# The opening of a fused attention and FFN kernel: loads in order of use, batch 0 in spare PSUM banks, dummy matmuls, FFN1 beside batch 1, and an ELU that reads PSUM once on VectorE

## The chip, the cores and the metric

One core of one Trainium2 chip. The metric is the device time of one execution in microseconds (us). Times are medians of several executions. The profile is that of one execution; its span runs from the first to the last instruction of the program and is about 2 us shorter than the device time.

"Clock" is the mean granted clock of TensorE, as a share of full speed.

## The reference

Attention over 8 batches, 8 heads, 576 queries of width 64, with 16 extra "beacon" keys and values in front of each sequence; causal for the ordinary keys. Its output, reshaped to 4608 tokens by 512, goes through a two-layer FFN with an ELU.

```python
k_all = concatenate([beacon_k, k], axis=2);  v_all = concatenate([beacon_v, v], axis=2)
scores = where(causal, -1e9, matmul(q, k_all.T) / sqrt(64))        # [8, 8, 576, 592]
a = softmax(scores);  attn = matmul(a, v_all)
x = attn.transpose(0, 2, 1, 3).reshape(4608, 512)
h = x @ w_in                                                        # 512 -> 2048
g = where(h > 0, h, exp(minimum(h, 0)) - 1)                         # ELU
out = g @ w_out                                                     # 2048 -> 512
```

## The kernel before

The heads of a batch are worked two at a time, as four "pairs". For a pair there are four steps: `T` transposes q and k on TensorE and copies them out of PSUM, `SC` makes a group of scores (four groups per pair, each with its Exp of 128x832 on ScalarE and its causal masks on VectorE), `AV` makes the product with v and, with a matrix of ones, the row sums, and normalises: ln and exp(-x) of the sums on ScalarE, then a multiply on VectorE. `AVR` does the last 64 queries of all four pairs.

The FFN takes tiles of 512 tokens. The kernel is a software pipeline: in a period, the attention of batch b, FFN1 of tile b-1 and FFN2 of tile b-2 are dealt out in 16 steps. Batch 0 has a period for itself, since no tile is ready; the next has batch 1 and FFN1 of tile 0; from then on all three run together. The instructions of an engine stand in the order of these calls, so the order of the calls is the schedule.

The kernel's PSUM tiles take eight banks: tag `S` two buffers of two banks, `hps` (FFN1) two of one, `ops` (FFN2) two of one.

```python
def T(b, p):
    t = psum.tile([P, 2, 1024], BF16, tag="S")
    ...                                      # 24 transposes of q and k into t
    nc.scalar.copy(out=qT..., in_=t[:, 0, 0:S]...)
    nc.scalar.copy(out=kT..., in_=t[:, 1, 0:S]...)

def AV(b, p):
    a = psum.tile([P, 2, 512], FP32, tag="S")
    av_mms(b, p, 0, Q1, a[:, 0, 0:Q1], a[:, 1, 0:Q1], True)   # v and ones by turns
    recip(rl, a[:, 1, 0:Q1])                                  # ScalarE: Ln, then Exp(-x)
    nc.vector.tensor_tensor(out=xT..., in0=a[:, 0, 0:Q1], in1=rl, op=ALU.mult)

def slots_of(b):
    for p in range(NP):
        sl.append(lambda p=p: (SC(b, p, 0), SC(b, p, 1)))
        sl.append(lambda p=p: (SC(b, p, 2), SC(b, p, 3)))
        sl.append(lambda p=p: (T(b, p + 1), AV(b, p)))        # last pair: AV, AVR
    if b + 1 < B: sl.append(lambda: T(b + 1, 0))

def ffn1(t, fc):
    ...                                      # 4 matmuls into hps
    nc.scalar.activation(out=e, in_=hps, func=AFT.Exp)
    nc.vector.tensor_scalar(out=r, in0=hps, scalar1=0.0, op0=ALU.max)
    nc.vector.scalar_tensor_tensor(out=gt, in0=e, scalar=1.0, in1=r,
                                   op0=ALU.subtract, op1=ALU.min)
# cut: loads, masks, ffn2, the loop over the periods
```

The softmax here doesn't subtract the row's maximum and nothing guards it: scores larger than these inputs give would overflow.

Of the kernel before, what the change touches and what calls it, by code (L numbers as in the profile page):

```python
# [17 lines left out]
def kernel(  # L18
# [11 lines left out]
    nc = tc.nc  # L30
# [80 lines left out]
    def load_v(b):  # L111
        v16 = st[b][2]
        nc.gpsimd.dma_start(
            out=v16[0:NB, 0, :, :], in_=beacon_v[b].rearrange("h n d -> n h d"))
        for j in range(NKC):
            r0 = NB if j == 0 else 0
            n = kc[j] - r0
            nc.gpsimd.dma_start(
                out=v16[r0:r0 + n, j, :, :],
                in_=v[b, :, ilo[j]:ilo[j] + n, :].rearrange("h s d -> s h d"),  # L120
            )

    bk32 = konst.tile([P, H, D], FP32)
    for b in range(B):
        nc.sync.dma_start(  # L125
            out=bk32[NB * b:NB * (b + 1), :, :],
            in_=beacon_k[b].rearrange("h n d -> n h d"))
    new_stage(0)
    load_qk(0, 0, 2)
    identb = konst.tile([P, P], BF16)  # L130
    make_identity(nc, identb)
    load_qk(0, 2, 4)
    triu = konst.tile([P, 2, P], FP16)
# [5 lines left out]
    ones = konst.tile([P, D], FP16)  # L139
    nc.gpsimd.memset(ones, 1.0)  # L140
    NKT = 3
    kTs = [konst.tile([P, P * NKC], BF16, name=f"kT{i}") for i in range(NKT)]
    for kt in kTs:
        nc.gpsimd.memset(kt[:, SK:P * NKC], 0.0)
    load_v(0)
    load_qk(0, 4, 8)
# [3 lines left out]
    new_stage(1)  # L150
    load_qk(1, 0, H)
    load_v(1)
# [3 lines left out]
    bkst = konst.tile([P, H, D], BF16)  # L156
    nc.vector.tensor_copy(out=bkst, in_=bk32)


    bkT = konst.tile([P, NP, P], BF16)  # L160

    def beacon_T():
        tb = psum.tile([P, 2, 1024], BF16, tag="S", name="tb")
        for p in range(NP):
            nc.tensor.transpose(
                out=tb[:, 0, P * p:P * (p + 1)], in_=bkst[:, 2 * p:2 * p + 2, :], identity=identb)
        nc.vector.tensor_copy(out=bkT, in_=tb[:, 0, 0:NP * P])
# [4 lines left out]
    def T(b, p):  # L172
        qst, kst, _ = st[b]
        t = psum.tile([P, 2, 1024], BF16, tag="S", name="tp")
        for i, src in ((0, qst), (1, kst)):
            for r in range(R):
                for h in range(2):
                    nc.tensor.transpose(  # L178
                        out=t[D * h:D * (h + 1), i, PR * r:PR * (r + 1)],
# [3 lines left out]
        qT = attn.tile([P, S], BF16, tag="qT")  # L183
        kT = kTs[(b * NP + p) % NKT]
        nc.vector.tensor_copy(out=kT[:, 0:NB], in_=bkT[:, p, NB * b:NB * (b + 1)])
        nc.scalar.copy(  # L186
            out=qT.rearrange("c (p r) -> c p r", r=R),
            in_=t[:, 0, 0:S].rearrange("c (r p) -> c p r", r=R))
        nc.scalar.copy(
            out=kT[:, NB:SK].rearrange("c (p r) -> c p r", r=R),  # L190
            in_=t[:, 1, 0:S].rearrange("c (r p) -> c p r", r=R))
        qkT[(b, p)] = (qT, kT)

    def SC(b, p, g):
        qT, kT = qkT[(b, p)]
        if g == 0:
            ets[(b, p)] = attn.tile([P, 2, ECOLS], FP16, tag="et", bufs=6, name="et")
        et = ets[(b, p)]
        s = psum.tile([P, 2, 512], FP32, tag="S", name="sc")
        c0, c1 = GW * g, GW * (g + 1)  # L200
# [24 lines left out]
    def av_mms(b, p, qa, qe, u, l, first):  # L225
        v16 = st[b][2]
        et = ets[(b, p)]
        for j in range(NKC):
# [5 lines left out]
            for dst, isl in ((u, False), (l, True)):  # L234
                for h in range(2):
                    nc.tensor.matmul(  # L236
                        out=dst[D * h:D * (h + 1), a - qa:qe - qa],
                        lhsT=ones[0:kc[j], :] if isl else v16[0:kc[j], j, 2 * p + h, :],
                        rhs=et[0:kc[j], h, ca:ce],
                        start=(first and j == 0),  # L240
                        stop=(j == NKC - 1 or ilo[j + 1] >= qe),
                        skip_group_check=True,
                    )

    def recip(o, i):
        nc.scalar.activation(out=o, in_=i, func=AFT.Ln, bias=0.0, scale=1.0)  # L246
# [122 lines left out]
```

## Time and profile before

| | before |
|---|---|
| median of 4 runs | 402.39 us (401.84 to 402.59) |
| span of the profiled run, clock | 400.2 us, 0.981 |
| TensorE, VectorE, ScalarE busy | 371.9, 282.4, 263.9 us |
| first transpose, first Exp of the scores | 9.38, 12.93 us |
| first FFN1 matmul of tile 0, of tile 1 | 43.55, 77.33 us |
| a period in the steady state | 41.75 us |

The engine names in the profile are PE for TensorE (PEld for its weight loads), ACT for ScalarE, DVE for VectorE and POOL for GpSimd.

The first view is the windows of the kernel before: each row is a stretch of time (from:to, its length), then the busy time of each engine with the number of its instructions, the granted clock, the DMA share and GB/s. I cut the stretches at the first Exp of each pair of batch 0, at the first FFN1 matmul of tile 0 and of tile 1, and at the end of the first full period.

```profile
core 0: us, PE busy (x) PEld busy (x) DVE busy (x) ACT busy (x) POOL busy (x), PEclk, DMA share, GB/s
12.93:20.01 7.08, 5.28 (x60) 3.53 (x57) 1.38 (x6) 5.44 (x8) 4.83 (x7) 1.00 1.21 176
20.01:27.63 7.62, 4.63 (x60) 3.51 (x60) 2.26 (x7) 5.54 (x10) 2.64 (x3) 0.78 1.25 206
27.63:34.92 7.29, 4.49 (x60) 3.28 (x60) 2.07 (x7) 5.53 (x9) 1.84 (x3) 0.77 1.61 189
34.92:43.55 8.63, 6.73 (x138) 5.64 (x138) 2.78 (x8) 5.26 (x9) 4.18 (x7) 0.60 1.51 196
43.55:77.33 33.78, 29.53 (x386) 15.38 (x385) 27.84 (x61) 31.38 (x52) 10.21 (x13) 1.00 1.05 122
77.33:119.08 41.75, 41.75 (x449) 20.85 (x448) 32.09 (x65) 32.02 (x51) 6.26 (x8) 1.00 0.59 69
```

The last row is the steady state: TensorE is busy in all of 41.75 us. The four pairs of batch 0 take 7 to 8.6 us each, in which TensorE is busy 4.5 to 6.7 us and ScalarE 5.3 to 5.5: neither is full, so waits bound the pairs. The clock falls to 0.60 there. With FFN1 of tile 0 beside batch 1, ScalarE is busy 31.4 of 33.8 us.

The second view is the timeline of ScalarE (start, length, engine, line, operation, output<-input, shapes, count; in brackets the idle time ahead and what ended it) between pair 0 and pair 1.

```profile
18.85 0.60 ACT L246 ACTIVATE rl<-av 128x512 f32<-128x512 f32 x1 [1.10 <-PE av L236]
19.48 0.63 ACT L247 ACTIVATE rl<-rl 128x512 f32<-128x512 f32 x1
20.01 0.84 ACT L216 ACTIVATE et<-sc 128x832 f16<-128x832 f32 x1
21.30 2.38 ACT L216 ACTIVATE et<-sc 128x832 f16<-128x832 f32 x3 [0.44 <-PE sc L208]
```

The second score group comes late: its Exp starts 1.29 us after the first, where the next follow at 0.76. Its bank of tag `S` held the product of pair 0 until VectorE's multiply had read it, which ended at 20.83. (The profile names the first Exp as what the scores waited for, since it ended 0.02 later.)

From the page's list of groups (busy us, mean ns of one | idle before, releaser): the two VectorE passes of the ELU, and the q copy on ScalarE.

```profile
L295 DVE TENSOR_SCALAR r<-hps 128x512 f16<-128x512 f32 x144 | 99.2, 689 | 23.1 <-ACT e L293 21.2
L297 DVE SCALAR_TENSOR_TENSOR gt<-e,r 128x512 f16<-128x512 f32 x144 | 99.7, 692 | 4.9
...
L186 ACT COPY qT<-tp 128x576 bf16<-128x576 bf16 x32 | 20.6, 643 | 25.0 <-PE tp L178 25.0
```

### The profile page before, as it was taken

What the parts mean: (1) busy time and instruction counts of PE and PEld (TensorE: products, weight loads), DVE (VectorE), ACT (ScalarE), POOL (GpSimd) and SP (SyncE); (2) the same over time, 40 slices, a digit from 0 to 9 for tenths busy, and PEclk for the clock granted to TensorE, in tenths of its full rate; (3) what the DMA queues carried; (4) which work ended last, traced back from release to release, by engine and by line L of the source; (5) the groups of instructions that cost most, each with busy time, mean ns of one, the idle gap of its engine ahead of it and who ended that gap; (6) DMA issues with size and microseconds to landing.
All of it is one profiled execution on the core that took longest, in us unless ns stands there. A gap on an engine that the chain in (4) does not pass through costs nothing.

```text
span 400.2 us, 8907 instructions
## 1 busy us (share of the span) xinstructions
PE 371.9 (93%) x3716; PEld 189.0 (47%) x3716; DVE 282.4 (71%) x558; ACT 263.9 (66%) x417; POOL 60.4 (15%) x88
## 2 busy tenths in 40 slices
PE   0656989999999999999999999999999999999996
PEld 0444644444554445444545454555455544444442
DVE  0132578977777777777787787777777788888841
ACT  1676899688758885788668875887588843333300
POOL 8734301400140014001400131000000000000000
PEclk9986899999999999999999999999999999999999
DMA  9999996900890079104950288000000001010112
GB/s 108 162 205 186 205 123 93 89 0 28 144 91 29 28 122 105 33 28 86 119 59 26 54 132 76 28 29 26 28 29 12 18 35 45 27 54 26 52 54 79
DMA packets 61864, 28.75 MB, mean 72 GB/s; under 512 B 40832, under 2 KB 57216, under 8 KB 61824
## 3 DMA queue, kind: packets, MB, share of 16 engines
q0 software_dynamic: 55488, 18.49, 41.8%
q1 hardware_dynamic: 6336, 9.70, 6.5%
q8 instruction: 29, 0.48, 0.5%
q14 instruction: 11, 0.09, 0.1%
HBM read 37.22 MB, written 9.44 MB: 117 GB/s over the span
## 4 chain that ended last, share of the span: by engine, by line
PE 87%; ACT 8%; DVE 2%; DMA 1%; SPq 1%; issue 0%; DVEq 0%
PE ops L309 31%; PE hps L288 31%; PE av L236 10%; PE sc L208 7%; PE tp L178 5%; ACT et L216 4%; PE avr L236 3%; DMA bk_82<-in_beacon_k_dram 1%; ACT rl L247 1%; ACT e L293 1%; ACT rl L246 1%; ACT qT L186 1%; SPq L125 1%; DVE xT L254 1%; DVE r L295 0%
## 5 line engine op out<-in xcount | busy, mean ns | idle before, releaser
L288 PE MATMUL hps<-xT,w_in_80 128*128 128x512 f16 x576 | 148.6, 381 | 1.0 <-DVE r L295 1.0
L309 PE MATMUL ops<-w_out_81,gt 128*128 128x512 f16 x576 | 145.2, 379 | 0.0
L293 ACT ACTIVATE e<-hps 128x512 f32<-128x512 f32 x144 | 86.2, 599 | 59.3 <-PE hps L288 58.0
L216 ACT ACTIVATE et<-sc 128x832 f16<-128x832 f32 x128 | 103.6, 862 | 18.6 <-PE sc L208 18.6
L295 DVE TENSOR_SCALAR r<-hps 128x512 f16<-128x512 f32 x144 | 99.2, 689 | 23.1 <-ACT e L293 21.2
L297 DVE SCALAR_TENSOR_TENSOR gt<-e,r 128x512 f16<-128x512 f32 x144 | 99.7, 692 | 4.9
L309 PEld LDWEIGHTS <-gt 128*128 128x128 f16 x576 | 56.3, 98 | 68.0
L288 PEld LDWEIGHTS <-w_in_80 128*128 128x128 f16 x576 | 48.9, 98 | 57.1 <-issue 6.3
L222 DVE TENSOR_TENSOR et<-et,triu 128x256 f16<-128x256 f16 (+2 forms) x160 | 39.4, 273 | 20.9 <-ACT et L216 20.7
L254 DVE TENSOR_TENSOR xT<-av,rl 128x512 f16<-128x512 f32 x32 | 22.1, 692 | 43.9 <-ACT rl L247 43.8
L236 PE MATMUL av<-et,ones 128*64 128x512 f16 (+4 forms) x320 | 39.3, 295 | 0.0
L186 ACT COPY qT<-tp 128x576 bf16<-128x576 bf16 x32 | 20.6, 643 | 25.0 <-PE tp L178 25.0
L236 PEld LDWEIGHTS <-ones 128*64 128x64 f16 (+1 forms) x640 | 31.7, 117 | 5.5 <-issue 0.8
L314 DVE COPY osb<-ops 128x512 f32<-128x512 f32 x36 | 24.7, 685 | 9.9 <-PE ops L309 9.9
L246 ACT ACTIVATE rl<-av 128x512 f32<-128x512 f32 x32 | 19.2, 600 | 12.3 <-PE av L236 12.3
L106 POOL DMA_DIRECT2D qst<-in_q_dram x10 | 7.6, 764 | 116.8 <-PE tp L178 116.0
L247 ACT ACTIVATE rl<-rl 128x512 f32<-128x512 f32 (+1 forms) x40 | 23.6, 589 | 1.3
L208 PE MATMUL sc<-qT,kT_108 64*128 64x208 bf16 (+5 forms) x176 | 13.9, 265 | 5.5 <-ACT et L216 3.4
L178 PEld LDWEIGHTS <-qst 96*64 96x64 bf16 x384 | 11.6, 117 | 12.9 <-issue 12.6
L208 PE MATMUL sc<-qT,kT_109 64*128 64x208 bf16 (+5 forms) x176 | 13.2, 254 | 3.8 <-ACT et L216 2.7
L178 PE MATMUL tp<-identb,qst 96*64 96x96 bf16 x384 | 15.5, 221 | 0.9 <-ACT et L216 0.8
L208 PE MATMUL sc<-qT,kT_110 64*128 64x208 bf16 (+5 forms) x160 | 12.0, 255 | 3.4 <-ACT et L216 2.6
(74 smaller groups left out, 237.3 us busy)
## 6 DMA issues: line engine op xcount, KB each, us to landing
out_dram<-osb SPq DMA_DIRECT2D x36, 256.0 KB, 2.0
qst<-in_q_dram POOLq DMA_DIRECT2D x7, 576.0 KB, 7.6
kst<-in_k_dram POOLq DMA_DIRECT2D x7, 576.0 KB, 9.8
w_in_80<-in_moe_w_in_dram POOLq DMA_DIRECT2D x4, 512.0 KB, 11.6
w_out_81<-in_moe_w_out_dram POOLq DMA_DIRECT2D x4, 512.0 KB, 10.8
v_93<-in_v_dram POOLq DMA_DIRECT2D x3, 128.0 KB, 4.0
v_128<-in_v_dram POOLq DMA_DIRECT2D x3, 128.0 KB, 13.2
v_602<-in_v_dram POOLq DMA_DIRECT2D x3, 128.0 KB, 12.8
```

Source lines behind the costliest of these rows:

```text
L178: nc.tensor.transpose(out=t[D * h:D * (h + 1), i, PR * r:PR * (r + 1)], in_=src[:, 2 * p + h, r, :], identity=identb[0:PR, 0:PR],)
L208: nc.tensor.matmul(out=s[:, h, a - c0:e - c0], lhsT=kT[D * h:D * (h + 1), P * j:P * (j + 1)], rhs=qT[D * h:D * (h + 1), qa:qa + e - a], st ...
L216: nc.scalar.activation(out=et[:, :, c0:c1], in_=s[:, :, 0:GW], func=AFT.Exp, bias=0.0, scale=SCALE)
L222: nc.vector.tensor_tensor(out=o, in0=o, in1=triu[0:kc[j], :, t0:t0 + w], op=ALU.mult)
L236: nc.tensor.matmul(out=dst[D * h:D * (h + 1), a - qa:qe - qa], lhsT=ones[0:kc[j], :] if isl else v16[0:kc[j], j, 2 * p + h, :], rhs=et[0:k ...
L247: nc.scalar.activation(out=o, in_=o, func=AFT.Exp, bias=0.0, scale=-1.0)
L254: nc.vector.tensor_tensor(out=xT[:, p, b * S:b * S + Q1], in0=a[:, 0, 0:Q1], in1=rl[:, 0:Q1], op=ALU.mult)
L288: nc.tensor.matmul(out=hps, lhsT=w_in16[:, cc, P * fc:P * (fc + 1)], rhs=xT[:, cc, TT * t:TT * (t + 1)], start=(cc == 0), stop=(cc == NCC ...
L293: nc.scalar.activation(out=e, in_=hps, func=AFT.Exp, bias=0.0, scale=1.0)
L295: nc.vector.tensor_scalar(out=r, in0=hps, scalar1=0.0, scalar2=None, op0=ALU.max)
L297: nc.vector.scalar_tensor_tensor(out=gt, in0=e, scalar=1.0, in1=r, op0=ALU.subtract, op1=ALU.min)
L309: nc.tensor.matmul(out=ops, lhsT=gts[(t, fc)][:, P * tb:P * (tb + 1)], rhs=w_out16[:, fc, :], start=(fc == 0), stop=(fc == NFC - 1))
```

## The change

The intent: fill the opening. Loads are issued in order of use and the beacon keys through two queues; in batch 0 the transposes use the banks of FFN1 and the products those of FFN2, both free at that time; dummy matmuls of zeros hold the TensorE clock up; pairs 0 and 1 have their scores made back to back; batch 1 starts early and its products come last; the q copies go to VectorE; the ELU reads PSUM once on VectorE (`max(h, min(e, 1) - 1)` instead of `min(e - 1, max(h, 0))`).

```diff
-    def T(b, p):
+    def T(b, p, early=False, kact=True):
+        if early:
+            tq, tk = bank("hps", BF16, "tq"), bank("hps", BF16, "tk")
...
-        nc.scalar.copy(out=qT..., ...)                  # and the k copy
+        (nc.scalar.copy if kact else nc.vector.tensor_copy)(out=kT..., in_=tk...)
+        nc.vector.tensor_copy(out=qT..., in_=tq...)
...
+    def AV(b, ps, early=False):
+        if early:
+            l, u = bank("ops", name="al"), bank("ops", name="au")
+        ...                                             # row sums (l) first, then v (u)
+        def norm(): ...                                 # Ln, Exp, multiply, when called
+        return norm
...
-        nc.vector.tensor_scalar(out=r, in0=hps, scalar1=0.0, scalar2=None, op0=ALU.max)
+        nc.vector.tensor_scalar(out=r, in0=e, scalar1=1.0, scalar2=1.0,
+                                op0=ALU.min, op1=ALU.subtract)
-        nc.vector.scalar_tensor_tensor(out=gt, in0=e, scalar=1.0, in1=r, ...)
+        nc.vector.tensor_tensor(out=gt, in0=hps, in1=r, op=ALU.max)
...
-    T(0, 0)
+    warm(w0, 12)                                        # 128x512 matmuls of zeros
+    beacon_T(); T(0, 0, True); T(0, 1, True, False)
+    SC(0, 0, 0, 1); SC(0, 0, 1, 1); SC(0, 0, 2, 1); SC(0, 0, 3, 1)   # last 1: one dummy
+    T(0, 2, True, False)
+    for g in range(4): SC(0, 1, g, 1)
+    T(0, 3, True, False)
+    n0 = AV(0, [0], True)
+    SC(0, 2, 0, 1); SC(0, 2, 1, 1); n0()
+    n1 = AV(0, [1], True)
+    SC(0, 2, 2, 1); SC(0, 2, 3, 1); n1()
+    ...                                                 # pair 3 alike
+    # FFN1 of tile 0: 16 steps with the rest of batch 1, its four AV and AVR last
+    # period 2: sl = [None] * 3 + [T(2, 0)] + the 13 slots as before
# cut: loads, memsets, the rest of the loop
```

More of the change, by code (lines that the diff above doesn't have):

```diff
@@ L109, in load_qk, with load_v @@
             )
-    def load_v(b):
+    def load_v(b, h0, h1):
         v16 = st[b][2]
-        nc.gpsimd.dma_start(
-            out=v16[0:NB, 0, :, :], in_=beacon_v[b].rearrange("h n d -> n h d"))
+        if h0 == 0:
+            nc.gpsimd.dma_start(
+                out=v16[0:NB, 0, :, :], in_=beacon_v[b].rearrange("h n d -> n h d"))
         for j in range(NKC):
@@ L118, in load_v @@
             nc.gpsimd.dma_start(
-                out=v16[r0:r0 + n, j, :, :],
-                in_=v[b, :, ilo[j]:ilo[j] + n, :].rearrange("h s d -> s h d"),
+                out=v16[r0:r0 + n, j, h0:h1, :],
+                in_=v[b, h0:h1, ilo[j]:ilo[j] + n, :].rearrange("h s d -> s h d"),
             )
@@ L124 @@
     for b in range(B):
-        nc.sync.dma_start(
+        (nc.sync if b % 2 == 0 else nc.scalar).dma_start(
             out=bk32[NB * b:NB * (b + 1), :, :],
             in_=beacon_k[b].rearrange("h n d -> n h d"))
+    zero = konst.tile([P, 512], BF16)
+    nc.vector.memset(zero, 0.0)
+    ones = konst.tile([P, D], FP16)
+    nc.vector.memset(ones, 1.0)
+    NKT = 3
+    kTs = [konst.tile([P, P * NKC], BF16, name=f"kT{i}") for i in range(NKT)]
+    for kt in kTs:
+        nc.vector.memset(kt[:, SK:P * NKC], 0.0)
+    identb = konst.tile([P, P], BF16)
+    triu = konst.tile([P, 2, P], FP16)
+    bkst = konst.tile([P, H, D], BF16)
+    bkT = konst.tile([P, NP, P], BF16)
     new_stage(0)
     load_qk(0, 0, 2)
-    identb = konst.tile([P, P], BF16)
     make_identity(nc, identb)
     load_qk(0, 2, 4)
-    triu = konst.tile([P, 2, P], FP16)
     nc.gpsimd.memset(triu, 1.0)
@@ L138 @@
     )
-    ones = konst.tile([P, D], FP16)
-    nc.gpsimd.memset(ones, 1.0)
-    NKT = 3
-    kTs = [konst.tile([P, P * NKC], BF16, name=f"kT{i}") for i in range(NKT)]
-    for kt in kTs:
-        nc.gpsimd.memset(kt[:, SK:P * NKC], 0.0)
-    load_v(0)
-    load_qk(0, 4, 8)
+    load_qk(0, 4, 6)
+    load_v(0, 0, 4)
+    load_qk(0, 6, 8)
+    load_v(0, 4, 8)
+    new_stage(1)
+    load_qk(1, 0, H)
     wi_v = moe_w_in.rearrange("(c p) f -> p c f", p=P)
@@ L149 @@
         nc.gpsimd.dma_start(out=w_in16[:, :, f0:f0 + 512], in_=wi_v[:, :, f0:f0 + 512])
-    new_stage(1)
-    load_qk(1, 0, H)
-    load_v(1)
+    load_v(1, 0, H)
     wo_v = moe_w_out.rearrange("(f p) m -> p f m", p=P)
@@ L155, with warm, bank @@
         nc.gpsimd.dma_start(out=w_out16[:, f0:f0 + 4, :], in_=wo_v[:, f0:f0 + 4, :])
-    bkst = konst.tile([P, H, D], BF16)
-    nc.vector.tensor_copy(out=bkst, in_=bk32)
-    bkT = konst.tile([P, NP, P], BF16)
+    def warm(t, n):
+        for _ in range(n):
+            nc.tensor.matmul(out=t, lhsT=zero[:, 0:P], rhs=zero, start=True, stop=True, skip_group_check=True)
+    def bank(tag, dt=FP32, name="bk"):
+        return psum.tile([P, 512 if dt == FP32 else 1024], dt, tag=tag, name=name)
     def beacon_T():
-        tb = psum.tile([P, 2, 1024], BF16, tag="S", name="tb")
+        tb = bank("hps", BF16, "tb")
+        nc.vector.tensor_copy(out=bkst, in_=bk32)
         for p in range(NP):
             nc.tensor.transpose(
-                out=tb[:, 0, P * p:P * (p + 1)], in_=bkst[:, 2 * p:2 * p + 2, :], identity=identb)
-        nc.vector.tensor_copy(out=bkT, in_=tb[:, 0, 0:NP * P])
+                out=tb[:, P * p:P * (p + 1)], in_=bkst[:, 2 * p:2 * p + 2, :], identity=identb)
+        nc.vector.tensor_copy(out=bkT, in_=tb[:, 0:NP * P])
     qkT = {}
     ets = {}
-    def T(b, p):
+    def T(b, p, early=False, kact=True):
         qst, kst, _ = st[b]
-        t = psum.tile([P, 2, 1024], BF16, tag="S", name="tp")
-        for i, src in ((0, qst), (1, kst)):
+        if early:
+            tq, tk = bank("hps", BF16, "tq"), bank("hps", BF16, "tk")
+        else:
+            t = psum.tile([P, 2, 1024], BF16, tag="S", name="tp")
+            tq, tk = t[:, 0, :], t[:, 1, :]
+        for dst, src in ((tq, qst), (tk, kst)):
             for r in range(R):
@@ L178, in T @@
                     nc.tensor.transpose(
-                        out=t[D * h:D * (h + 1), i, PR * r:PR * (r + 1)],
+                        out=dst[D * h:D * (h + 1), PR * r:PR * (r + 1)],
                         in_=src[:, 2 * p + h, r, :],
@@ L182, in T, with SC @@
                     )
-        qT = attn.tile([P, S], BF16, tag="qT")
+        qT = attn.tile([P, S], BF16, tag="qT", bufs=3)
         kT = kTs[(b * NP + p) % NKT]
         nc.vector.tensor_copy(out=kT[:, 0:NB], in_=bkT[:, p, NB * b:NB * (b + 1)])
-        nc.scalar.copy(
+        (nc.scalar.copy if kact else nc.vector.tensor_copy)(
+            out=kT[:, NB:SK].rearrange("c (p r) -> c p r", r=R),
+            in_=tk[:, 0:S].rearrange("c (r p) -> c p r", r=R))
+        nc.vector.tensor_copy(
             out=qT.rearrange("c (p r) -> c p r", r=R),
-            in_=t[:, 0, 0:S].rearrange("c (r p) -> c p r", r=R))
-        nc.scalar.copy(
-            out=kT[:, NB:SK].rearrange("c (p r) -> c p r", r=R),
-            in_=t[:, 1, 0:S].rearrange("c (r p) -> c p r", r=R))
+            in_=tq[:, 0:S].rearrange("c (r p) -> c p r", r=R))
         qkT[(b, p)] = (qT, kT)
-    def SC(b, p, g):
+    def SC(b, p, g, nwarm=0):
         qT, kT = qkT[(b, p)]
         if g == 0:
-            ets[(b, p)] = attn.tile([P, 2, ECOLS], FP16, tag="et", bufs=6, name="et")
+            ets[(b, p)] = attn.tile([P, 2, ECOLS], FP16, tag="et", bufs=5, name="et")
         et = ets[(b, p)]
         s = psum.tile([P, 2, 512], FP32, tag="S", name="sc")
+        warm(s[:, 0, :], nwarm)
         c0, c1 = GW * g, GW * (g + 1)
@@ L223, in SC, with av_mms @@
                 out=o, in0=o, in1=triu[0:kc[j], :, t0:t0 + w], op=ALU.mult)
-    def av_mms(b, p, qa, qe, u, l, first):
+    def av_mms(b, p, qa, qe, dst, isl, first):
         v16 = st[b][2]
@@ L233, in av_mms @@
             ce = ca + qe - a
-            for dst, isl in ((u, False), (l, True)):
-                for h in range(2):
-                    nc.tensor.matmul(
-                        out=dst[D * h:D * (h + 1), a - qa:qe - qa],
-                        lhsT=ones[0:kc[j], :] if isl else v16[0:kc[j], j, 2 * p + h, :],
-                        rhs=et[0:kc[j], h, ca:ce],
-                        start=(first and j == 0),
-                        stop=(j == NKC - 1 or ilo[j + 1] >= qe),
-                        skip_group_check=True,
-                    )
@@ L245, in recip @@
-    def recip(o, i):
-        nc.scalar.activation(out=o, in_=i, func=AFT.Ln, bias=0.0, scale=1.0)
-        nc.scalar.activation(out=o, in_=o, func=AFT.Exp, bias=0.0, scale=-1.0)
-    def AV(b, p):
-        a = psum.tile([P, 2, 512], FP32, tag="S", name="av")
-        av_mms(b, p, 0, Q1, a[:, 0, 0:Q1], a[:, 1, 0:Q1], True)
-        rl = attn.tile([P, 512], FP32, tag="rl")
-        recip(rl[:, 0:Q1], a[:, 1, 0:Q1])
-        nc.vector.tensor_tensor(
-            out=xT[:, p, b * S:b * S + Q1], in0=a[:, 0, 0:Q1], in1=rl[:, 0:Q1], op=ALU.mult)
@@ L257, in AVR @@
-    def AVR(b):
-        a = psum.tile([P, 2, 512], FP32, tag="S", name="avr")
-        for p in range(NP):
-            av_mms(b, p, Q1, S, a[:, 0, QR * p:QR * (p + 1)], a[:, 1, QR * p:QR * (p + 1)], p == 0)
-        w = NP * QR
-        rl = attn.tile([P, 512], FP32, tag="rl")
-        recip(rl[:, 0:w], a[:, 1, 0:w])
-        nc.vector.tensor_tensor(
-            out=xT[:, :, b * S + Q1:(b + 1) * S],
-            in0=a[:, 0, 0:w].rearrange("c (p q) -> c p q", p=NP),
-            in1=rl[:, 0:w].rearrange("c (p q) -> c p q", p=NP), op=ALU.mult)
+            for h in range(2):
+                nc.tensor.matmul(
+                    out=dst[D * h:D * (h + 1), a - qa:qe - qa],
+                    lhsT=ones[0:kc[j], :] if isl else v16[0:kc[j], j, 2 * p + h, :],
+                    rhs=et[0:kc[j], h, ca:ce],
+                    start=(first and j == 0),
+                    stop=(j == NKC - 1 or ilo[j + 1] >= qe),
+                    skip_group_check=True,
+                )
@@ new lines, in AV, with norm @@
+    def AV(b, ps, early=False):
+        if early:
+            l, u = bank("ops", name="al"), bank("ops", name="au")
+        else:
+            a = psum.tile([P, 2, 512], FP32, tag="S", name="av")
+            l, u = a[:, 0, :], a[:, 1, :]
+        qa, qe = (0, Q1) if len(ps) == 1 else (Q1, S)
+        n = qe - qa
+        w = n * len(ps)
+        for dst, isl in ((l, True), (u, False)):
+            for i, p in enumerate(ps):
+                av_mms(b, p, qa, qe, dst[:, n * i:n * (i + 1)], isl, i == 0)
+        def norm():
+            rl = attn.tile([P, 512], FP32, tag="rl")
+            nc.scalar.activation(out=rl[:, 0:w], in_=l[:, 0:w], func=AFT.Ln, bias=0.0, scale=1.0)
+            nc.scalar.activation(out=rl[:, 0:w], in_=rl[:, 0:w], func=AFT.Exp, bias=0.0, scale=-1.0)
+            nc.vector.tensor_tensor(
+                out=xT[:, ps[0]:ps[-1] + 1, b * S + qa:b * S + qe],
+                in0=u[:, 0:w].rearrange("c (p q) -> c p q", q=n),
+                in1=rl[:, 0:w].rearrange("c (p q) -> c p q", q=n), op=ALU.mult)
+        return norm
@@ L269, in slots_of @@
+    ALL = list(range(NP))
     def slots_of(b):
@@ L274, in slots_of @@
             if p + 1 < NP:
-                sl.append(lambda p=p: (T(b, p + 1), AV(b, p)))
+                sl.append(lambda p=p: (T(b, p + 1), AV(b, [p])()))
             else:
-                sl.append(lambda p=p: (AV(b, p), AVR(b)))
+                sl.append(lambda p=p: (AV(b, [p])(), AV(b, ALL)()))
         if b + 1 < B:
@@ L294, in ffn1 @@
         r = melt.tile([P, TT], FP16, tag="r")
-        nc.vector.tensor_scalar(out=r, in0=hps, scalar1=0.0, scalar2=None, op0=ALU.max)
+        nc.vector.tensor_scalar(
+            out=r, in0=e, scalar1=1.0, scalar2=1.0, op0=ALU.min, op1=ALU.subtract)
         gt = gpool.tile([P, TT], FP16, tag="g", name="gt")
-        nc.vector.scalar_tensor_tensor(
-            out=gt, in0=e, scalar=1.0, in1=r, op0=ALU.subtract, op1=ALU.min)
+        nc.vector.tensor_tensor(out=gt, in0=hps, in1=r, op=ALU.max)
         gts[(t, fc)] = gt
@@ L316, in ffn2 @@
             nc.sync.dma_start(out=out[row:row + P, :], in_=osb)
+    w0 = bank("ops", name="w0")
+    warm(w0, 12)
     beacon_T()
-    T(0, 0)
-    for period in range(NTT + 2):
-        b, t1, t2 = period, period - 1, period - 2
-        if 0 < b and b + 1 < B:
+    T(0, 0, True)
+    T(0, 1, True, False)
+    SC(0, 0, 0, 1)
+    SC(0, 0, 1, 1)
+    SC(0, 0, 2, 1)
+    SC(0, 0, 3, 1)
+    T(0, 2, True, False)
+    for g in range(4):
+        SC(0, 1, g, 1)
+    T(0, 3, True, False)
+    n0 = AV(0, [0], True)
+    SC(0, 2, 0, 1)
+    SC(0, 2, 1, 1)
+    n0()
+    n1 = AV(0, [1], True)
+    SC(0, 2, 2, 1)
+    SC(0, 2, 3, 1)
+    n1()
+    SC(0, 3, 0, 1)
+    SC(0, 3, 1, 1)
+    n2 = AV(0, [2], True)
+    SC(0, 3, 2, 1)
+    SC(0, 3, 3, 1)
+    n2()
+    T(1, 0)
+    n3 = AV(0, [3], True)
+    n3()
+    n4 = AV(0, ALL, True)
+    SC(1, 0, 0)
+    n4()
+    SC(1, 0, 1)
+    sl = [lambda: (SC(1, 0, 2), SC(1, 0, 3)), lambda: T(1, 1)]
+    for p in range(1, NP):
+        sl.append(lambda p=p: (SC(1, p, 0), SC(1, p, 1)))
+        sl.append(lambda p=p: (SC(1, p, 2), SC(1, p, 3)))
+        if p + 1 < NP:
+            sl.append(lambda p=p: T(1, p + 1))
+    for p in range(NP):
+        sl.append(lambda p=p: AV(1, [p], True)())
+    sl.append(lambda: AV(1, ALL, True)())
+    for i in range(NFC):
+        ffn1(0, i)
+        if i < len(sl):
+            sl[i]()
+    for s_ in sl[NFC:]:
+        s_()
+    for period in range(2, NTT + 2):
+        b, t1, t2 = period, period - 1, period - 2
+        first = 0
+        if b == 2:
+            new_stage(2)
+            load_qk(2, 0, H)
+            load_v(2, 0, H)
+        if b + 1 < B:
             new_stage(b + 1)
             load_qk(b + 1, 0, H)
-            load_v(b + 1)
+            load_v(b + 1, 0, H)
         sl = slots_of(b) if b < B else []
-        if t1 < 0:
-            for s in sl:
-                s()
-            continue
+        if b == 2:
+            sl = [None] * 3 + [lambda: T(2, 0)] + sl
         for i in range(NFC):
@@ L334 @@
                 ffn1(t1, i)
-            if t2 >= 0:
-                ffn2(t2, i)
-            if i < len(sl):
+            ffn2(t2, i)
+            if i < len(sl) and sl[i] is not None:
                 sl[i]()
+        for s_ in sl[NFC:]:
+            s_()
 _INS = ['q', 'k', 'v', 'beacon_k', 'beacon_v', 'moe_w_in', 'moe_w_out']
```

## The prediction

> **What bounds the kernel now.** The windows view shows TensorE busy 10.00 of every 10 us from 80 us to 390 us at clock 1.00. In the chain of waits the period there is 41.75 us (avr pieces at 110.20, 151.95, 193.70): 128 FFN matmuls of about 0.216 us are 27.6 us, one batch's attention the rest. Nothing that only helps VectorE or ScalarE can shorten it. What can shrink is the first 77.3 us, up to the first FFN1 matmul of tile 1. There the timeline shows: beacon keys land at 8.8, first transpose 9.4, first softmax Exp 12.9; then 7.6 us per head pair (Exp starts 12.9, 20.0, 27.6, 35.0), because products and normalisation are chained with the next scores; first FFN1 matmul 43.55; FFN1 of tile 0 beside batch 1 takes 33.8 us, paced by ScalarE (9.8 of 10 busy) and at its end by VectorE (9.1). The granted clock flips between 0.5 and 1.0 until 43.5 us; a pair of 512-column products takes 0.42 us cold, 0.22 warm.
>
> **The change, costed.**
> - Beacon loads on two queues (eight issues of 0.46 us in a row before), fewer GpSimd memsets: first transpose near 7.2. But two head pairs are now transposed before the first scores, so the first Exp starts near 11.3 (1.6 us earlier).
> - Pairs 0 and 1: scores run back to back, 0.8 us per Exp of 128x832, 3.6 us per pair instead of 7.6. This is the main gain, about 8 us.
> - Pairs 2 and 3 gain nothing: the product of pair p+1 writes the two banks that pair p's Ln (0.60) and final multiply (0.69) must first read, and later scores stand behind it in TensorE's order. About 8 us each, ScalarE idle about 2 us after a normalisation. First FFN1 matmul: 36.6 if warm, 38.5 if half cold.
> - FFN1 of tile 0 beside batch 1: ScalarE loses the q copies (0.64 each), but the q copy queues on VectorE behind the ELU and the next scores wait for it; five product slots come last at 2.2 us each on TensorE. I sum 33 to 34 us, as before.
> - The transposes of batch 2 move into the next period: 0.75 us more there.
> - ELU: the first VectorE pass reads SBUF instead of PSUM. The Trainium skill, "VectorE: DVE Perf Modes" (Mode 2x_2P), lets a one-source fp32 operation from SBUF make two results per cycle, and not from PSUM. This trace agrees: the 128x512 f32 cast from SBUF took 0.43 us, the copy from PSUM 0.69. So 144 x 0.26 = 37 us of VectorE, off the critical path.
> - Dummy matmuls keep the clock up ("TensorE: Matmul & The Clock Gate", Part 1); counted above, worth 0 to 3 us.
>
> FFN1 of tile 1 starts near 71.5 instead of 77.3: 5.8 earlier, 0.75 given back, 1 us off for slack in my sums: 402.4 to about 396.
>
> **Prediction: 396 us, 389 to 400.5.** Faster by over 2%: 0.40; within 2%: 0.57; slower: 0.03.
>
> **What would show it.** Exp starts of pairs 0 to 3 near 11, 15, 20, 28; first FFN1 matmul 36 to 39; FFN1 of tile 1 at 70 to 73; period still 41.7; ELU's SBUF pass near 0.43 us; VectorE busy down by 20 to 35 us.
>
> **What would make it wrong.** The clock staying warm and batch 1 overlapping better (390 or less); loads of heads 6 and 7 landing after 17 us; FFN1's banks, held longer now, stalling TensorE in the last periods (up to 2 us).

## The result, and the profile after

| | before | after |
|---|---|---|
| median (4 runs each) | 402.39 us | 397.58 us (396.05 to 398.40) |
| ratio of the runs, 95% interval | | 0.9878 (0.9843 to 0.9913) |
| span of the profiled run, clock | 400.2 us, 0.981 | 394.3 us, 0.998 |
| first transpose, first Exp | 9.38, 12.93 us | 6.35, 9.76 us |
| first FFN1 matmul of tile 0, of tile 1 | 43.55, 77.33 us | 34.81, 69.37 us |
| TensorE, VectorE, ScalarE busy | 371.9, 282.4, 263.9 us | 375.0, 274.1, 245.3 us |

A ratio is the mean time of one kernel's runs over that of the other's in the same rounds, so it is not quite the ratio of the medians quoted. The gain is 1.2%, inside 2%. The profiled run of the changed kernel is its fastest; two of the four runs took 398.2 and 398.4 us.

The windows of the changed kernel, cut at the same events as before, columns as above:

```profile
9.76:13.37 3.61, 3.17 (x45) 1.44 (x44) 2.01 (x7) 3.24 (x5) 3.61 (x7) 1.00 1.48 112
13.37:18.44 5.07, 4.53 (x65) 2.35 (x64) 4.04 (x12) 3.24 (x5) 5.07 (x8) 1.00 1.38 110
18.44:26.08 7.64, 4.98 (x51) 2.45 (x52) 2.04 (x7) 5.38 (x9) 4.70 (x7) 1.00 1.27 198
26.08:34.81 8.73, 6.42 (x160) 4.65 (x157) 4.11 (x10) 6.06 (x11) 2.40 (x4) 1.00 1.31 202
34.81:69.37 34.56, 28.24 (x356) 14.39 (x355) 27.47 (x62) 28.41 (x46) 10.83 (x14) 1.00 1.34 164
69.37:113.05 43.68, 42.62 (x474) 21.38 (x472) 32.27 (x72) 30.16 (x47) 6.92 (x10) 1.00 0.48 66
```

Against before: the first Exp comes 3.2 us earlier, pairs 0 to 2 take 16.3 us instead of 22.0 together, the last pair up to FFN1 8.7 as before (8.6), FFN1 of tile 0 34.6 instead of 33.8, and the first full period 43.7 instead of 41.75. Later periods are equal (41.77 us). The sum, -3.2 -5.7 +0.1 +0.8 +1.9, is -6.1 by these rounded steps; the span is 5.9 us shorter.

The timeline of all engines in pair 2 shows a new wait (other lines left out):

```profile
18.44 1.62 ACT L233 ACTIVATE et<-sc 128x832 f16<-128x832 f32 x2 [1.83 <-PE sc L225]
...
18.93 0.11 PEld L252 LDWEIGHTS <-ones 128*64 128x64 f16 x1 [0.17 <-issue]
...
19.94 0.60 ACT L278 ACTIVATE rl<-al 128x512 f32<-128x512 f32 x1
...
20.58 0.63 ACT L279 ACTIVATE rl<-rl 128x512 f32<-128x512 f32 x1
20.60 0.77 PE L252 MATMUL al<-et,ones 128*64 128x512 f16 x10 [1.59 <-ACT rl L278]
...
21.24 0.69 DVE L280 TENSOR_TENSOR xT<-au,rl 128x512 f16<-128x512 f32 x1 [0.86 <-ACT rl L279]
21.99 0.76 PE L252 MATMUL au<-et,v_107 128*64 128x512 f16 x10 [0.62 <-DVE xT L280]
...
22.68 0.39 PE L168 MATMUL sc<-zero 128*128 128x512 bf16 x1
...
23.01 0.35 PE L225 MATMUL sc<-qT,kT_97 64*128 64x208 bf16 x4
...
23.40 1.62 ACT L233 ACTIVATE et<-sc 128x832 f16<-128x832 f32 x2 [2.19 <-PE sc L225]
```

The row sums of pair 1 (`al` at 20.60) go into the bank that the Ln of pair 0 must first read, so they wait 1.59 us; the product (`au` at 21.99) waits for the multiply of pair 0. The scores of pair 2 stand behind both in TensorE's order, so ScalarE idles 2.19 us before 23.40. The Trainium skill, "TensorE: Matmul & The Clock Gate" (Part 2), says of this engine: "The MATMULs themselves stay in program order — the reorder is *only* the LDWEIGHTS pull-ahead". The trace agrees: the weights of the row sums were loaded at 18.93, 1.67 us ahead of their matmul, and no matmul passed it.

The groups of the ELU and of the q copy after:

```profile
L317 DVE TENSOR_TENSOR gt<-hps,r 128x512 f16<-128x512 f32 x144 | 99.6, 692 | 5.0
...
L314 DVE TENSOR_SCALAR r<-e 128x512 f16<-128x512 f32 x144 | 62.1, 431 | 32.8 <-ACT e L312 31.5
...
L205 DVE COPY qT<-tp 128x576 bf16<-128x576 bf16 x28 | 21.2, 757 | 1.8 <-ACT kT_95 L202 0.9
```

The pass that now reads SBUF takes 431 ns instead of 689, as the cast of the same size did before. The q copy costs VectorE 757 ns.

The chain of waits (start, length, what) at the end of the first full period:

```profile
109.04 1.32 PE av L252 x20
...
110.38 0.60 ACT rl L278
...
111.01 0.64 ACT rl L279
...
111.67 0.70 DVE xT L280
...
112.42 0.70 PE tp L194 x24
```

In that period batch 2 has 17 slots (the first three empty), so its last products and the transposes after them fall at the very end. Those transposes wait for the bank that the product holds until its multiply.

### The profile page after: what moved, and what is told of

Read it like the earlier page. It is cut to its first block, busy times and chain, and to the rows that moved or that the text cites. A ratio compares the mean times of both kernels' runs of the same rounds, so it can differ in the third digit from the quotient of the medians.

```text
span 394.3 us, 8966 instructions
## 1 busy us (share of the span) xinstructions
PE 375.0 (95%) x3743; PEld 184.8 (47%) x3744; DVE 274.1 (70%) x598; ACT 245.3 (62%) x382; POOL 64.4 (16%) x91
## 4 chain that ended last, share of the span: by engine, by line
PE 88%; ACT 6%; DVE 4%; issue 1%
PE hps L307 31%; PE ops L328 31%; PE av L252 9%; PE sc L225 7%; ACT et L233 4%; PE tp L194 4%; PE au L252 2%; PE w_152 L168 1%; DVE xT L280 1%; DVE gt L317 1%; PE al L252 1%; ACT e L312 1%; ACT rl L279 1%; ACT rl L278 1%; DVE r L314 1%
## 5 line engine op out<-in xcount | busy, mean ns | idle before, releaser
L317 DVE TENSOR_TENSOR gt<-hps,r 128x512 f16<-128x512 f32 x144 | 99.6, 692 | 5.0
L314 DVE TENSOR_SCALAR r<-e 128x512 f16<-128x512 f32 x144 | 62.1, 431 | 32.8 <-ACT e L312 31.5
L239 DVE TENSOR_TENSOR et<-et,triu 128x256 f16<-128x256 f16 (+2 forms) x160 | 40.8, 275 | 32.8 <-ACT et L233 32.1
L280 DVE TENSOR_TENSOR xT<-av,rl 128x512 f16<-128x512 f32 (+1 forms) x30 | 19.1, 638 | 24.0 <-ACT rl L279 24.0
L252 PEld LDWEIGHTS <-ones 128*64 128x64 f16 (+1 forms) x640 | 21.7, 111 | 12.3 <-issue 7.2
L278 ACT ACTIVATE rl<-av 128x512 f32<-128x512 f32 (+1 forms) x30 | 16.6, 554 | 17.1 <-PE av L252 17.0
L252 PE MATMUL av<-et,ones 128*64 128x64 f16 (+6 forms) x480 | 22.8, 237 | 0.0
L205 DVE COPY qT<-tp 128x576 bf16<-128x576 bf16 x28 | 21.2, 757 | 1.8 <-ACT kT_95 L202 0.9
L194 PEld LDWEIGHTS <-qst 96*64 96x64 bf16 x384 | 10.3, 109 | 13.3 <-issue 12.9
L225 PE MATMUL sc<-qT,kT_95 64*128 64x208 bf16 (+5 forms) x176 | 13.4, 252 | 2.0 <-DVE qT L205 1.5
L194 PE MATMUL tp<-identb,qst 96*64 96x96 bf16 x336 | 12.5, 210 | 1.1 <-DVE xT L280 0.8
```

Of the source, the lines that this page charges most:

```text
L194: nc.tensor.transpose(out=dst[D * h:D * (h + 1), PR * r:PR * (r + 1)], in_=src[:, 2 * p + h, r, :], identity=identb[0:PR, 0:PR],)
L225: nc.tensor.matmul(out=s[:, h, a - c0:e - c0], lhsT=kT[D * h:D * (h + 1), P * j:P * (j + 1)], rhs=qT[D * h:D * (h + 1), qa:qa + e - a], st ...
L239: nc.vector.tensor_tensor(out=o, in0=o, in1=triu[0:kc[j], :, t0:t0 + w], op=ALU.mult)
L252: nc.tensor.matmul(out=dst[D * h:D * (h + 1), a - qa:qe - qa], lhsT=ones[0:kc[j], :] if isl else v16[0:kc[j], j, 2 * p + h, :], rhs=et[0:k ...
L314: nc.vector.tensor_scalar(out=r, in0=e, scalar1=1.0, scalar2=1.0, op0=ALU.min, op1=ALU.subtract)
L317: nc.vector.tensor_tensor(out=gt, in0=hps, in1=r, op=ALU.max)
```

## The experiments

Each kernel was timed in alternation with the kernel before, on one chip, and gave a right result. "Order" is the order of calls of batch 0. Of these, u_order, m_banks and best2 are faster than the kernel before by over 2% with their whole interval. Runs against the kernel before are compared with its runs on the same chip; runs against each other by medians, with the ratios in the table as the check.

| run | what it is | median, us | ratio to before (95%) |
|---|---|---|---|
| (the change) | | 397.58 | 0.9878 (0.9843 to 0.9913) |
| u_nowarm | change, no dummies | 398.77 | 0.9910 (0.9897 to 0.9924) |
| u_oldelu | change, old ELU | 397.61 | 0.9875 (0.9859 to 0.9891) |
| u_order | change, old order | 393.39 | 0.9778 (0.9765 to 0.9792) |
| u_order_cold | the same, no dummies | 395.32 | 0.9824 (0.9811 to 0.9837) |
| r_actcopy | u_order, copies of batch 0 on ScalarE | 393.47 | 0.9789 (0.9775 to 0.9804) |
| m_banks | change, two more banks | 391.59 | 0.9734 (0.9720 to 0.9747) |
| b_warm | before + dummies | 399.98 | 0.9952 (0.9930 to 0.9974) |
| b_spare | before + spare banks | 399.98 | 0.9950 (0.9934 to 0.9966) |
| b_both | before + both | 396.19 | 0.9854 (0.9830 to 0.9878) |
| m_tearly | change, transposes of batch 1 earlier | 395.85 | 0.9842 (0.9829 to 0.9854) |
| m_t2back | change, transposes of batch 2 moved back | 396.79 | 0.9873 (0.9858 to 0.9887) |
| best2 | change, four mends | 389.59 | 0.9692 (0.9678 to 0.9706) |

### Is the new order the gain? (u_order)

```diff
-    ...                             # pairs 0 and 1 back to back, products later
+    for p in range(NP):
+        for g in range(4):
+            SC(0, p, g, 1)
+        T(0, p + 1, True, False)    # after pair 3: T(1, 0)
+        AV(0, [p], True)()
+    AV(0, ALL, True)()
+    SC(1, 0, 0)
+    SC(1, 0, 1)
```

Expected:

> The changed kernel with batch 0 in the order of the kernel before (scores of a pair, transposes of the next, its products, normalisation, then the next pair); all else stays: spare banks, dummies, loads, q copies on VectorE. If running pairs 0 and 1 back to back is the main gain, Exp starts are again about 7 us apart for all four pairs, the first FFN1 matmul comes at 38 to 39 instead of 34.8 and the time is 401 us. If the warm clock alone made the opening faster, the pairs are 5.5 to 6 us apart and the time stays at 396 to 399.

Measured: 393.39 us, 4.2 us *faster* than the change by medians (its slowest run, 393.65, is under the change's fastest, 396.05), and outside both ranges of time; the spacing of the pairs is that of the second alternative. Its windows, cut at the first Exp of each pair and at the FFN1 matmuls, columns as above:

```profile
8.92:14.47 5.55, 4.88 (x65) 2.58 (x64) 2.96 (x9) 4.46 (x6) 5.55 (x9) 1.00 1.47 128
14.47:20.03 5.56, 4.81 (x65) 2.50 (x64) 3.40 (x10) 4.46 (x6) 5.56 (x9) 1.00 1.38 125
20.03:25.59 5.56, 4.81 (x65) 2.50 (x64) 3.40 (x10) 4.46 (x6) 2.32 (x4) 1.00 1.28 201
25.59:32.85 7.26, 5.97 (x148) 3.94 (x147) 3.69 (x10) 5.98 (x10) 2.48 (x3) 1.00 1.25 207
32.85:66.69 33.84, 28.18 (x356) 14.29 (x355) 27.02 (x62) 27.72 (x44) 11.57 (x15) 1.00 1.45 177
```

In the old order the pairs are an even 5.56 us apart. Three pairs take 16.7 us, against 16.3 in the new order: what the new order wins on pairs 0 and 1 it loses on pair 2. It then loses more: its last pair takes 8.73 us against 7.26, its first Exp comes 0.84 later because two pairs are transposed first, and FFN1 of tile 0 takes 34.56 against 33.84. So the shorter pairs come from something that both have. The new order as it stands is a loss: these steps make up the 2.6 us of difference between the two profiled runs (391.7 and 394.3 us), of which the change's is its fastest.

### The clock, by itself and with the rest (u_nowarm, b_warm, u_order_cold)

u_nowarm leaves out all dummy matmuls of the change.

```diff
     def warm(t, n):
-        for _ in range(n):
+        for _ in range(0):
```

> The changed kernel without any dummy matmul. My theory (the order of the opening is the main gain, the clock worth 0 to 3 us): first FFN1 matmul 1 to 3 us later than 34.8, the time 398 to 401 us. Rival (the clock is the main gain): the opening falls back to half clock, first FFN1 matmul at 38 or later, 401 us or more, nearly all of the gain gone. Rival 2 (the dummies only cost TensorE time): 395 to 397.

Measured: 398.77 us, 1.2 us slower than the change, by ratios whose intervals overlap; in its trace the first FFN1 matmul comes at 37.30 instead of 34.81. The clock is not the main gain of the change.

b_warm adds nothing but dummies to the kernel before:

```diff
+    w0 = psum.tile([P, 512], FP32, tag="ops", name="w0")
+    warm(w0, 16)
     beacon_T()
...
         s = psum.tile([P, 2, 512], FP32, tag="S", name="sc")
+        warm(s[:, 0, :], 1 if b == 0 else 0)
```

> The kernel before with nothing but the dummy matmuls: 16 ahead of the first transpose and one before each score group of batch 0. The run with the old order of batch 0 refuted my step that pairs 0 and 1 back to back are the main gain. New theory: the clock is. Warm, the transposes of a pair take 0.6 us instead of 1.2 and its products 1.2 instead of 2.3, so a pair takes about 5.9 us instead of 7.5, the first FFN1 matmul comes at 36 to 38 instead of 43.55, and the time is 395 to 398: as much as the whole change. Rival (the spare banks and the q copies on VectorE shortened the pair): the pair stays above 7 us, the time above 400.

Measured: 399.98 us, a gain of 2.1; the runs spread from 399.13 to 402.11, with clocks of 0.990 to 0.977. The theory falls. In its trace the pairs are still 7.3 to 7.7 us apart, as the rival said, and the first FFN1 matmul comes at 43.66. Its profile is of the slowest of the six runs: there the clock record is at 0.5 from 9.9 to 20.2 us and in two later windows of 3.41 us. In the old banks the waits remain, and dummies that stand behind a wait don't fill it: the dummy of pair 1's second score group starts at 21.99, after TensorE had idled 1.35 us.

u_order_cold is u_order without dummies.

> The changed kernel with the old order of batch 0 and no dummy matmuls. If the clock is the main gain: pairs about 7 us apart again, first FFN1 matmul 5 us or more later than with the dummies (32.85), time 397.5 to 400. If the banks and copies are: pairs stay at 5.6 to 6 us and the time at 394 to 395.

Measured: 395.32 us, 1.9 us slower than u_order (the intervals of the ratios are apart). First FFN1 matmul at 34.46 instead of 32.85. Pairs are 5.9, 5.4 and 5.6 us apart even so, the second alternative of what was expected (the time is 0.3 us above its range), and the clock still dips in two windows (21.7 to 25.2 and 28.6 to 32.0). So 6.8 of the 9.1 us are there without dummies.

### The spare banks and the copies (b_spare, r_actcopy, b_both)

b_spare adds to the kernel before only the banks: in batch 0, transposes in `hps`, products in `ops`.

```diff
-        t = psum.tile([P, 2, 1024], BF16, tag="S", name="tp")
+        if b == 0:
+            tt = [psum.tile([P, 1024], BF16, tag="hps", name=n) for n in ("tq", "tk")]
...
+    def pair(b, name):
+        if b == 0:
+            return [psum.tile([P, 512], FP32, tag="ops", name=name) for _ in range(2)]
```

> The kernel before with one part of the change alone: in batch 0 the transposes use the two banks of FFN1 and the products the two banks of FFN2, instead of sharing the score banks. Old order, no dummies, copies on ScalarE, loads as before. Since the old order with the rest of the change but no dummies ran at 395.3 us, and the dummies alone at 400, the theory now is that the spare banks are the largest part: the second score group of a pair no longer waits for the multiply of the pair before (1.3 us of ScalarE idle before the second Exp, four times), pairs 6 to 6.5 us apart instead of 7.5, first FFN1 matmul 3 to 5 us earlier, time 397.5 to 399.5. Rival (moving the copies off ScalarE, or the loads, is the largest part): 401 or more.

Measured: 399.98 us, a gain of 2.4, just short of the expected 399.5. The wait named in the expectation is gone: the four Exp of pair 1 start at 18.93, 19.68, 20.42, 21.17, where before the second came 1.3 us after the first. Pairs are 6.8, 5.3 and 6.5 us apart, and the first FFN1 matmul comes at 40.51, 3.0 earlier.

r_actcopy puts the q and k copies of batch 0 in u_order back on ScalarE.

```diff
-        nc.vector.tensor_copy(
+        (nc.scalar.copy if b == 0 else nc.vector.tensor_copy)(
             out=qT.rearrange(...), ...)
-            T(0, p + 1, True, False)
+            T(0, p + 1, True, True)
```

> The changed kernel with the old order of batch 0 (393.4 us) and, in batch 0 alone, both copies of a pair on ScalarE as before instead of VectorE. If the copies are a large part of the gain, the four pairs take 6.2 us or more instead of 5.56 and the time is 395.5 or more; if the spare banks carry it, ScalarE, idle while the products run, takes the copies for at most 0.3 us a pair: 393.3 to 394.8.

Measured: 393.47 us, against 393.39. Moving the copies off ScalarE is worth nothing in batch 0: in this trace the pairs are 5.36 us apart instead of 5.56, and the first Exp comes 0.44 later (9.36).

b_both adds both parts to the kernel before, banks and dummies. (The text recorded for it says that each gave 2.4 us alone; the dummies gave 2.1.)

> The kernel before with two parts of the change, the spare banks for batch 0 and the dummy matmuls (24 at the start, since its beacon keys land later, and one before each score group of batch 0). Alone each gave 2.4 us. Theory: together they give more than their sum, because the dummies keep the clock up only where TensorE has no longer waits, and the banks take the long waits out: the clock stays at 1.0, pairs are 5.6 us apart as in the old order of the changed kernel, first FFN1 matmul at 36 to 37.5, time 395 to 396.5 (6 us or more gained). The rest down to 393.4 us is then the earlier first Exp. Rival (independent parts): the clock still falls in windows of the opening, pairs above 6 us, 397.3 to 398.5.

Measured: 396.19 us, 5.7 us less than its run of the kernel before. The two parts alone gave 2.1 and 2.4, so together they give about 1.2 us more than their sum, which is near the noise; its opening has one window at half clock (34.1 to 37.5) where the kernel before had four. Its windows, cut at the first Exp of each pair and at the first FFN1 matmul, columns as above:

```profile
12.38:17.76 5.38, 4.90 (x69) 2.54 (x69) 1.43 (x6) 5.35 (x9) 4.60 (x8) 1.00 1.27 180
17.76:23.12 5.36, 4.34 (x64) 2.33 (x64) 2.08 (x7) 5.33 (x9) 1.48 (x2) 1.00 1.24 207
23.12:28.48 5.36, 4.34 (x64) 2.33 (x64) 2.07 (x7) 5.33 (x9) 1.75 (x2) 1.00 1.27 205
28.48:37.64 9.16, 6.24 (x136) 4.54 (x136) 2.68 (x7) 5.18 (x9) 4.58 (x7) 0.81 1.78 183
```

Three pairs are 5.4 us apart each, with ScalarE busy in 5.33 of 5.36 us: here it, and no longer a wait, is the limit. The time is inside the theory's range (395 to 396.5); the gain is just short of its 6 us, the first FFN1 matmul a little later than its 37.5, and the clock did fall once. These two parts, in the old order, gain about as much as the whole change does (the intervals overlap).

### The wait that the new order brought (m_banks)

```diff
+            tag = "hps" if b == 0 and ps in ([1], [3]) else "ops"
-            l, u = bank("ops", name="al"), bank("ops", name="au")
+            l, u = bank(tag, name="al"), bank(tag, name="au")
```

> The changed kernel with the products of pairs 1 and 3 of batch 0 in the other two spare banks (those of the early transposes, free by then), so that they don't wait for the Ln and the multiply of the pair before. My theory: ScalarE no longer idles 2 us after a normalisation, pairs 2 and 3 take 4.5 to 5.5 us instead of 7.6 and 8.7, the first FFN1 matmul comes 4 to 6 us earlier (29 to 31) and the time is 391 to 394. Rival (the pairs are held up by the work of ScalarE or by loads, the bank wait being only the last to end): under 1.5 us, 396 or more.

Measured: 391.59 us, 6.0 us faster than the change by medians; the profiled runs, of which the change's is its fastest, are 4.4 us apart. Pair 2 takes 5.33 us, as expected, and pair 3 takes 6.36, more than expected. First FFN1 matmul at 29.93 instead of 34.81; its four runs lie within 0.3 us of each other, all at clock 1.00. Its timeline at the same place:

```profile
18.24 1.62 ACT L233 ACTIVATE et<-sc 128x832 f16<-128x832 f32 x2 [1.54 <-PE sc L225]
...
18.73 0.77 PE L252 MATMUL al<-et,ones 128*64 128x512 f16 x10
...
19.35 0.74 PE L252 MATMUL au<-et,v 128*64 128x512 f16 x10
19.74 0.60 ACT L279 ACTIVATE rl<-al 128x512 f32<-128x512 f32 x1
...
20.38 0.63 ACT L280 ACTIVATE rl<-rl 128x512 f32<-128x512 f32 x1
...
20.92 1.60 ACT L233 ACTIVATE et<-sc 128x832 f16<-128x832 f32 x2
```

The row sums of pair 1 run at 18.73, before the Ln of pair 0 has even started, and the next Exp follows the normalisation at once (20.92). That is the new order with what it needs: here it beats the old order (393.39).

The change's opening appears unchanged in three other kernels (u_oldelu, m_tearly, m_t2back). In the profile of each, the clock record has a window at 0.5 that starts between 21.2 and 22.1 us, in the stretch where TensorE waits for the banks, and the first FFN1 matmul comes at 35.3 to 35.6. The run of the change that was profiled escaped this. It may be part of the change's spread of 2.4 us, but that is not shown: in these three traces the first FFN1 matmul comes only 0.45 to 0.75 us later, so the rest of the spread stays open. The runs of b_both, which has two bank waits left ahead of its window at half clock (0.69 and 1.17 us, in the work on the last 64 queries), spread over 3.3 us, those of u_order and m_banks over 0.3.

### The ELU (u_oldelu)

```diff
-        nc.vector.tensor_scalar(out=r, in0=e, scalar1=1.0, scalar2=1.0, op0=ALU.min, op1=ALU.subtract)
+        nc.vector.tensor_scalar(out=r, in0=hps, scalar1=0.0, scalar2=None, op0=ALU.max)
-        nc.vector.tensor_tensor(out=gt, in0=hps, in1=r, op=ALU.max)
+        nc.vector.scalar_tensor_tensor(out=gt, in0=e, scalar=1.0, in1=r, op0=ALU.subtract, op1=ALU.min)
```

> The changed kernel with the old ELU (both VectorE passes at 0.69 us, one more from PSUM). My theory: VectorE is busy 37 us more but off the critical path, time within 1 us of the changed kernel (397 to 399). Rival: beside batch 1 the q copy stands behind the ELU on VectorE, three pairs of passes of 0.26 us each and the wait for qT grows, so FFN1 of tile 1 starts 2 us or more later and the time is 399.5 or more.

Measured: 397.61 us, against 397.58. VectorE is busy 305.7 us instead of 274.1, and by medians it costs nothing. But the trace shows a little of what the rival named: beside batch 1 the scores of a pair wait 1.76 us for the q copy instead of 1.49, two pairs are 6.7 us apart instead of 6.5, and FFN1 of tile 0 takes 36.43 us instead of 34.56, with a window at half clock in it (55.7 to 59.1). That profile is of the slowest of the five runs; a loss of up to about 1 us could hide in the spread of the two kernels.

### Two small losses (m_tearly, m_t2back)

m_tearly moves the transposes of each next pair of batch 1 forward, between the two score slots of the pair ahead of it.

```diff
         sl.append(lambda p=p: (SC(1, p, 0), SC(1, p, 1)))
+        if p + 1 < NP:
+            sl.append(lambda p=p: T(1, p + 1))
         sl.append(lambda p=p: (SC(1, p, 2), SC(1, p, 3)))
-        if p + 1 < NP:
-            sl.append(lambda p=p: T(1, p + 1))
```

> The changed kernel with the transposes of the next pair of batch 1 one slot earlier, between its two score slots, so that the q copy on VectorE is done before the scores want it. My theory: the two waits of 1.49 us of the scores on the q copy go, a pair takes about 5.2 us instead of 6.5, FFN1 of tile 1 starts 2 to 3 us earlier relative to the first FFN1 matmul (34.56 now), time 394.5 to 396. Rival (ScalarE or VectorE work bounds this stretch): under 0.8 us.

Measured: 395.85 us, 1.7 less than the change; the ratios' intervals overlap a little. FFN1 of tile 0 takes 33.61 us instead of 34.56, so 0.95 of the 2 to 3 expected. The wait has partly moved: the Exp of the second score slot now comes late (43.43, then 45.91 us).

m_t2back puts the transposes of batch 2 back into the last slot beside batch 1.

```diff
+    sl.append(lambda: T(2, 0))              # after AVR of batch 1
...
-        if b == 2:
-            sl = [None] * 3 + [lambda: T(2, 0)] + sl
```

> The changed kernel with the transposes of batch 2 back in the last slot beside batch 1, so that the next period has 16 slots again. My theory: that period falls from 43.7 to about 41.8 us (0.63 of transposes moved out, and the last transposes no longer wait 0.8 us for the bank of a product), the stretch before gets 0.7 longer: 1.0 to 1.4 us gained in all, 396.2 to 396.8. Rival: the same work elsewhere, no change (397.3 to 398).

Measured: 396.79 us, 0.8 less, by medians alone within the noise. The traces show it: the period takes 42.10 instead of 43.68 us, the stretch before it 35.28 instead of 34.56. The net is 0.9 less, just below what was expected.

### All mends together (best2)

The three mends above and one more: `T(0, 1)` after the first two score groups instead of ahead of them.

> The changed kernel with four mends together: products of pairs 1 and 3 in the other two spare banks, the transposes of pair 1 after the first two score groups of pair 0, the transposes of batch 1 one slot earlier, those of batch 2 back beside batch 1. By the single runs 391.6 less 0.8 (first Exp at 8.9 instead of 9.8) less 1.0 to 1.7 less 0.8: 388.3 to 389.5. If the mends hide one another (the loads of the FFN1 weights land at 28 to 36 us and would hold an earlier FFN1), 390 or more.

Measured: 389.59 us, 8.0 less than the change and 12.8 less than the kernel before: it beats both. It is just above the range. The first Exp comes at 9.02 instead of m_banks' 9.85, but pair 1 starts at 13.51 instead of 13.46 and the first FFN1 matmul at 29.98 instead of 29.93, so that mend brought nothing. No wait of TensorE on the weight loads shows in its trace.

## Why the prediction was right or wrong

The predicted time was 396 us (389 to 400.5); measured were 397.58, and 1.2% is inside the 2% that was held most likely. Point by point:

- **"Nothing that only helps VectorE or ScalarE can shorten it."** Right of the steady state, of which it was said: later periods are 41.77 us (before 41.75), with the old ELU too, and its median time was the same (397.61).
- **"Pairs 0 and 1: scores run back to back ... This is the main gain, about 8 us."** This step failed, though its description of the trace was good (3.61 us from pair 0 to pair 1, predicted 3.6; Exp starts at 9.8, 13.4, 18.4, 26.1, predicted 11, 15, 20, 28). It compared the new order with the old order *in the kernel before*. The old order in the changed kernel takes 5.56 us a pair and ends 4.2 us earlier (u_order). What shortened the pairs is the spare banks, with the dummies on top (b_both: 5.7 us of gain in the old order). The order as it stood was a loss. The 8 us are not in the prediction's own starts either, which put pair 2 at 5 us after pair 1 and not 3.6; the two pairs took 3.61 and 5.07 us, 6.0 less than before.
- **"Pairs 2 and 3 gain nothing": about 8 us each, ScalarE idle about 2 us.** Right, and the cause is shown: 7.64 and 8.73 us, idle 2.19, and with other banks both this idle time and 6.0 us of the total (4.4 between the profiled runs) are gone (m_banks). The prediction booked this as no gain; it also made the order a loss, since the old order needs no such wait.
- **First Exp at 11.3.** Mis-sized: 9.76. The transposes began at 6.35, not 7.2, and were not held up further.
- **FFN1 of tile 0 "33 to 34 us, as before".** Nearly right: 34.56 (before 33.78). The wait for the q copy exists (1.49 us for each of the last two pairs), but taking it away gave only 0.95 us in the trace.
- **"0.75 us more" for the transposes of batch 2.** Mis-sized: 1.93 us. The sum counted the transposes, and not that a 17th slot pushes the last product to the end of the period, where its bank is waited for; moved back, the period is 42.10.
- **VectorE busy "down by 20 to 35 us".** Wrong: 8.3. The SBUF pass fell from 99.2 to 62.1 us in all, the 37 predicted; the q copies, which the same text moves to VectorE, were left out of that line (28 of them are 21.2 us).
- **Dummies "worth 0 to 3 us".** Right: 1.2 us in the new order (intervals overlap), 1.9 in the old.

That the total came within 2 us of the forecast is in part luck: it rested on a wrong account of the main gain, and the errors cancelled in part. The first Exp came 1.5 us earlier than predicted; the first full period was 1.2 us longer, and the median run is 1.5 us slower than the profiled one, whose clock of 0.998 the other three (0.991 to 0.996) did not reach.

What stays open: b_both ends at 396.19 and u_order at 393.39. u_order has the first Exp 3.5 us earlier (8.92 against 12.38 us), since its first transpose starts at 6.43 instead of 9.93. From there to the first FFN1 matmul it takes 23.93 us against 25.26, where b_both has its window at half clock, and it loses 1.9 in the first full period. No run takes out the loads, the early start of batch 1 or the row sums made ahead of the products by themselves.

## What to carry to other kernels

Test an order of work against the old order *with the other parts of the change in place*; a gain that is read as "before against after" can belong to what came with it. Before moving a product ahead in an in-order engine, ask which bank it writes and who must read that bank first, since everything behind it will wait too: two more banks made the same order 6 us faster. Dummy work didn't hold the clock where the waits stayed (b_warm: three windows in a row at 0.5); with the waits mostly gone the clock held through the opening in the profiles of u_order and m_banks, and fell once in b_both's.

## What the Trainium skill lacked or had wrong

- "TensorE: Matmul & The Clock Gate" (Part 1) gives the window of the clock gate as 3413 ns and two levels for it. The clock records agree (windows of 3.413 us or multiples, the last of a run aside, at 0.5 or 1.0). It doesn't say how busy a window must be to keep the clock: here the clock fell to 0.5 during the bank waits of pair 2 in the profiles of three kernels, and not in a fourth with the same opening, where TensorE was busy 4.98 of 7.64 us there, dummies included.
- No page says that the granted clock is shown as 1.00 until its first record. In the kernel before that record comes at 19.6 us; the windows view says 1.00 for 12.93 to 20.01, while pairs of 512-column products took 0.42 us there, as in a stretch of 0.5 (0.22 when warm).
- "ScalarE: Activation LUTs" (What ACT_TABLE_LOAD costs) has the load at about 1283 ns; the trace agrees (1.28 us). It doesn't say that the engine's queue can issue DMAs meanwhile: the first beacon load was issued from it at 0.83 us, 0.03 after the table load had begun.
- "DMA: Bandwidth & Descriptors" (Anatomy of one DMA) fits 2.0 us plus bytes over 436 GB/s for loads from GpSimd. By that fit, as an estimate, a load of q for one pair (144 KB) takes 2.3 us (2.7 if the 288 KB of fp32 that it reads are counted); here it took 4.2 in the median, with other loads in flight and a cast to bf16.
